# Moving the stores of a streaming add to a second DMA ring, with a smaller last chunk

## Chip, core and metric

The kernel runs on one core of one Trainium2 chip. The time is device microseconds from start to end of one execution. The profile's "span" leaves out a part of the launch, so it is about 1.8 us shorter than the time of the same execution (before: span 150.6 us, time 152.39 us).

## The reference

```python
# B, S, D = 512, 32, 640, bfloat16; alpha has one element
def reference(x, fx, alpha):
    return x + alpha * fx
```

Two arrays of 20.97 MB are read and one is written: 62.92 MB in all, and one multiply-add per element.

## The kernel before

The arrays are seen as 128 partitions of 81,920 columns, cut into five chunks of 16,384 columns (4 MB per array, 32 KB per partition row). Chunk k has an x tile (four buffers) and an f tile (two buffers); the result overwrites the x tile and is stored from it. In this text x2 is the load of x for chunk 2, f2 that of fx, c2 its compute, s2 its store; counting starts at 0, so "the third store" is s2. A "ring" is the queue of transfers of one issuing engine. Before, everything but alpha goes through one ring, that of SyncE:

```python
    load_x(0); load_f(0); load_x(1); load_f(1); load_x(2)
    compute(0)
    load_f(2);  store(0);  load_x(3)
    compute(1)
    load_f(3);  store(1);  load_x(4)
    compute(2)
    load_f(4);  store(2)
    compute(3)
    store(3)
    compute(4, 2)                     # last chunk in two halves
    store(4, 0, 2);  store(4, 1, 2)
    # (joined onto fewer lines here; compute is one VectorE instruction, or two halves)
```

## Time and profile before

| | before |
|---|---|
| time, median of 3 runs | 153.1 us (152.6 to 153.13) |
| span of the profile | 150.6 us |
| DMA engines moving data | 98.0% of the span = 147.6 us |
| DMA engines not moving data | 150.6 - 147.6 = 3.0 us |
| VectorE busy | 86.9 us (58%) |

DMA engines are the 16 units that move data between the chip's memory and the core. These are lines of the profile page of before. In the rows DVE (VectorE) and DMA each of the 40 figures stands for one fortieth of the span (3.8 us) and gives the busy share in tenths; the GB/s row gives what the DMA engines moved in it. A queue line gives packets, MB, and the time of its packets as a share of the span of the 16 DMA engines; q1 is the SyncE ring, q10 the ScalarE ring.

```profile
span 150.6 us, 85 instructions
...
DVE  0000009999679998499991006999900089997000
...
DMA  6999999999999999799999999999999999999994
GB/s 200 444 453 435 418 418 418 418 444 453 444 453 435 418 418 418 339 444 470 418 418 418 418 418 435 435 435 453 426 435 444 418 418 435 435 435 405 426 444 205
...
q1 hardware_dynamic: 2304, 62.92, 98.0%
q10 hardware_dynamic: 2, 0.00, 0.0%
```

DMA is at 9 in all but the first, last and one middle slice, while VectorE has long zeros. The bytes are fixed, so the DMA engines' rate bounds the kernel, and only the 3.0 us in which they do not work could be saved. Nearly all of these lie at the two ends: by the packet records, 1.7 us pass before the first row starts, and 1.2 us after the last one has ended.

The next lines are from the timeline of before (start us, duration us, engine, line, instruction, and in brackets how long the engine had been idle and what ended that).

```profile
62.24 17.28 DVE L69 SCALAR_TENSOR_TENSOR x_t<-f_t,a_f,x_t 128x16384 bf16<-128x16384 bf16 x1 [2.71 <-DMA f_t<-in_fx_dram]
...
120.91 17.42 DVE L69 SCALAR_TENSOR_TENSOR x_t<-f_t,a_f,x_t 128x8192 bf16<-128x8192 bf16 x2 [11.91 <-DMA f_t<-in_fx_dram]
```

The last load, f4, is in just before 120.91 us, and 17.42 us of compute follow. They cost nothing, because two whole stores (s2 and s3) stand in the ring behind f4 and keep the DMA engines busy while VectorE works.

### The profile page before, as it was taken

What the parts mean: (1) busy time and instruction counts of PE and PEld (TensorE: products, weight loads), DVE (VectorE), ACT (ScalarE), POOL (GpSimd) and SP (SyncE); (2) the same over time, 40 slices, a digit from 0 to 9 for tenths busy, and PEclk for the clock granted to TensorE, in tenths of its full rate; (3) what the DMA queues carried; (4) which work ended last, traced back from release to release, by engine and by line L of the source; (5) the groups of instructions that cost most, each with busy time, mean ns of one, the idle gap of its engine ahead of it and who ended that gap; (6) DMA issues with size and microseconds to landing.
All of it is one profiled execution on the core that took longest, in us unless ns stands there. A gap on an engine that the chain in (4) does not pass through costs nothing.

```text
span 150.6 us, 85 instructions
## 1 busy us (share of the span) xinstructions
PE 0.2 (0%) x1; PEld 0.1 (0%) x1; DVE 86.9 (58%) x8; POOL 0.2 (0%) x4
## 2 busy tenths in 40 slices
PE   0000000000000000000000000000000000000000
PEld 0000000000000000000000000000000000000000
DVE  0000009999679998499991006999900089997000
POOL 0000000000000000000000000000000000000000
DMA  6999999999999999799999999999999999999994
GB/s 200 444 453 435 418 418 418 418 444 453 444 453 435 418 418 418 339 444 470 418 418 418 418 418 435 435 435 453 426 435 444 418 418 435 435 435 405 426 444 205
DMA packets 2306, 62.92 MB, mean 418 GB/s; under 512 B 258, under 2 KB 258, under 8 KB 258
## 3 DMA queue, kind: packets, MB, share of 16 engines
q1 hardware_dynamic: 2304, 62.92, 98.0%
q10 hardware_dynamic: 2, 0.00, 0.0%
HBM read 41.94 MB, written 20.97 MB: 418 GB/s over the span
## 4 chain that ended last, share of the span: by engine, by line
DMA 56%; DVE 29%; DVEq 6%; issue 0%; SPq 0%
DMA f_t<-in_fx_dram 56%; DVE x_t L69 29%; DVEq L131 6%; SPq L59 0%; DVEq L69 0%
## 5 line engine op out<-in xcount | busy, mean ns | idle before, releaser
L69 DVE SCALAR_TENSOR_TENSOR x_t<-f_t,a_f,x_t 128x16384 bf16<-128x16384 bf16 (+1 forms) x6 | 86.6, 14439 | 49.5 <-DMA f_t<-in_fx_dram 49.5
L26 DVE COPY a_f<-a_ps 128x1 f32<-128x1 f32 x1 | 0.2, 159 | 1.1 <-PE a_ps L24 1.1
L22 DVE MEMSET ones<- 1x128 bf16 x1 | 0.2, 165 | 0.8 <-PEq L120 0.8
L24 PE MATMUL a_ps<-a,ones 1*128 1x1 bf16 x1 | 0.2, 159 | 1.9 <-DMA a<-in_alpha_dram 1.9
L120 POOL MEMSET const-bfloat16-1.0<- 128x1 bf16 x1 | 0.1, 102 | 0.0
L120 POOL MEMSET const-uint8-127<- 128x1 uint8 x1 | 0.1, 102 | 0.0
L24 PEld LDWEIGHTS <-ones 1*128 1x128 bf16 x1 | 0.1, 100 | 1.0 <-DVE ones L22 1.0
L120 POOL MEMSET const-float32-0.0<- 128x1 f32 x1 | 0.1, 99 | 0.2 <-issue 0.2
L120 POOL MEMSET const-float32-1.0<- 128x1 f32 x1 | 0.1, 99 | 0.0
## 6 DMA issues: line engine op xcount, KB each, us to landing
x_t<-in_x_dram SPq DMA_DIRECT2D x5, 4096.0 KB, 34.8
f_t<-in_fx_dram SPq DMA_DIRECT2D x5, 4096.0 KB, 32.1
out_dram<-x_t SPq DMA_DIRECT2D x4, 4096.0 KB, 36.5
out_dram<-x_t SPq DMA_DIRECT2D x2, 2048.0 KB, 15.2
a<-in_alpha_dram ACTq DMA_DIRECT2D x1, 0.0 KB
```

What stands on the lines that cost most here:

```text
L22: nc.vector.memset(ones[:], 1.0)
L24: nc.tensor.matmul(a_ps[:], ones[:], a_1[:], start=True, stop=True)
L26: nc.vector.tensor_copy(out=a_f[:], in_=a_ps[:])
L69: nc.vector.scalar_tensor_tensor(out=xt[k][:, s], in0=ft[k][:, s], scalar=a_f[:], in1=xt[k][:, s], op0=ALU.mult, op1=ALU.add,)
L120: nc = _bacc.Bacc("TRN2", target_bir_lowering=False, num_devices=1)
L131: with _tile.TileContext(nc) as tc:
```

## The change

The intent is to serve stores in rotation with loads, from a ring of their own, and to make the last chunks smaller so that less compute is left at the end. Only the third store is held, until the load f3 has landed. The diff, cut to its core:

```diff
-CHUNK = 16384
+SIZES = [16384, 16384, 16384, 16384, 8192, 8192]
 ...
-        nc.sync.dma_start(out=ov[...], in_=xt[k][:, bass.ts(j, n)])
+        st = nc.scalar.dma_start(out=ov[:, a : a + n], in_=xt[k][:, bass.ts(j, n)])
+        if behind is not None:
+            tc.add_manual_dep(st.ins, landed[behind].ins.name, ...)   # landed[k]: load_f(k)
 ...
     compute(2)
     load_f(4)
-    store(2)
+    load_x(5)
+    store(2, behind=3)
     compute(3)
+    load_f(5)
     store(3)
-    compute(4, 2)
-    store(4, 0, 2)
-    store(4, 1, 2)
+    compute(4)
+    store(4)
+    compute(5, 0, 2)
+    store(5, 0, 2)
+    compute(5, 1, 2)
+    store(5, 1, 2)
```

More of the change, by code (lines that the diff above doesn't have):

```diff
@@ L11 @@
 BF16 = mybir.dt.bfloat16
-CHUNK = 16384
+SIZES = [16384, 16384, 16384, 16384, 8192, 8192]
+STARTS = [sum(SIZES[:k]) for k in range(len(SIZES))]
+SLOT = max(SIZES)
 def alpha_to_lanes(nc, consts, psum, alpha, eng):
@@ L44 @@
     F = xv.shape[1]
-    K = F // CHUNK
-    assert K * CHUNK == F and K == 5
+    assert sum(SIZES) == F
     consts = ctx.enter_context(tc.tile_pool(name="consts", bufs=1))
@@ L54, with compute, store @@
     a_f = alpha_to_lanes(nc, consts, psum, alpha, nc.scalar)
-    xt, ft = {}, {}
+    xt, ft, landed = {}, {}, {}
     def load_x(k):
-        xt[k] = xs.tile([P, CHUNK], x.dtype, tag="x", name="x_t")
-        nc.sync.dma_start(out=xt[k][:], in_=xv[:, bass.ts(k, CHUNK)])
+        xt[k] = xs.tile([P, SLOT], x.dtype, tag="x", name="x_t")
+        nc.sync.dma_start(out=xt[k][:, : SIZES[k]], in_=xv[:, STARTS[k] : STARTS[k] + SIZES[k]])
     def load_f(k):
-        ft[k] = fs.tile([P, CHUNK], fx.dtype, tag="f", name="f_t")
-        nc.sync.dma_start(out=ft[k][:], in_=fxv[:, bass.ts(k, CHUNK)])
-    def compute(k, parts=1):
-        n = CHUNK // parts
-        for j in range(parts):
-            s = bass.ts(j, n)
-            nc.vector.scalar_tensor_tensor(
-                out=xt[k][:, s],
-                in0=ft[k][:, s],
-                scalar=a_f[:],
-                in1=xt[k][:, s],
-                op0=ALU.mult,
-                op1=ALU.add,
-            )
-    def store(k, j=0, parts=1):
-        n = CHUNK // parts
-        nc.sync.dma_start(
-            out=ov[:, k * CHUNK + j * n : k * CHUNK + (j + 1) * n],
-            in_=xt[k][:, bass.ts(j, n)],
-        )
+        ft[k] = fs.tile([P, SLOT], fx.dtype, tag="f", name="f_t")
+        landed[k] = nc.sync.dma_start(
+            out=ft[k][:, : SIZES[k]], in_=fxv[:, STARTS[k] : STARTS[k] + SIZES[k]]
+        )
+    def compute(k, j=0, parts=1):
+        n = SIZES[k] // parts
+        s = bass.ts(j, n)
+        nc.vector.scalar_tensor_tensor(
+            out=xt[k][:, s],
+            in0=ft[k][:, s],
+            scalar=a_f[:],
+            in1=xt[k][:, s],
+            op0=ALU.mult,
+            op1=ALU.add,
+        )
+    def store(k, j=0, parts=1, behind=None):
+        n = SIZES[k] // parts
+        a = STARTS[k] + j * n
+        st = nc.scalar.dma_start(out=ov[:, a : a + n], in_=xt[k][:, bass.ts(j, n)])
+        if behind is not None:
+            tc.add_manual_dep(
+                st.ins,
+                landed[behind].ins.name,
+                mybir.DependencyInfo(mybir.DependencyClass.Sync, mybir.DependencyReason.DATA),
+                reason="store behind a later load",
+            )
     load_x(0)
```

## The prediction

> **What bounds the kernel now.** The 16 DMA engines. The queue table gives the one data queue 98.0% of the 16 engines' span; the 40 slices show DMA at 9 in nearly every slice; 62.92 MB move in 150.6 us. A window of loads alone (10 to 20 us) runs at 433 GB/s, and the trace's packet records show one 32 KB row taking 1.213 us on its engine. Fifteen transfers of 4 MB are 15 x 8 x 1.213 = 145.6 us; with 1.7 us before the first byte, a slow first row, completion writes between transfers and about 1.2 us after the last, that is all of the span. VectorE is busy 86.9 us (58%) and hidden; the chain of waits runs through f landings and compute only because the single ring is always full. So there is at most about 1 us to gain, and anything that empties the rings costs time one for one.
>
> **What the change does.** Bytes are the same. Rows of 16 KB take 0.611 us (trace, last stores), so halving the last chunk costs about 0.3 us. Issue time moves from SyncE to the ScalarE queue (0.33 to 0.67 us each) and was never limiting. The Trainium skill, "DMA: Bandwidth & Descriptors", section "Issuing engines are not separate DMA queues", says transfers from both queues run on the same 16 engines and interleave; so I expect no bandwidth from the second ring (no trace here shows two rings yet).
>
> What changes is order. Before, the ring keeps two 4 MB stores (19.5 us of work) queued behind the last load, f4, which lands at 120.7 us; they cover both half computes (8.75 us each), and DMA never idles. After, each store is served while its following loads are: it takes its share early, f2 lands near 80 us instead of 62.2 (waits on f landings grow), later loads are late, and little store work is left behind the last load.
>
> I replayed both programs with these durations, one engine, issue-to-data 1.2 us, last-row-to-wait 1.1 us. The replay of before gives 149.8 us (measured 150.6). For after it depends on how an engine shares two rings, which this trace does not show:
> - a row from each in turn (32 KB store rows then get two thirds against 16 KB load rows): 158.3. The last load lands at 144.5, s3 and s4 are done by 145; then DMA idles about 6 us for the first 4.4 us half compute and issue, 2 us more before the last store.
> - a whole transfer in turn: 154.0, idle about 4 us at the tail.
> - bytes shared equally: 151.5, idle 1.5 us.
>
> The skill's same page, "Queues, rings and completion order", says engines round-robin between queues by packet, which fits the first or second best. Holding the third store behind f3 changes only the third case.
>
> **Prediction.** Adding 0.8 us of replay error and the 2.5 us between span and median time (153.1 less 150.6) gives 161.6, 157.3 and 154.8 us. I predict 157.5 us, 153.0 to 162.5 eight times in ten. Faster by over 2%: 0.02; within 2%: 0.42; slower by over 2%: 0.56.
>
> **What would show it.** Two data queues, DMA share falling from 98% to 93-96% with the loss in the last two or three of the 40 slices and 9s before; VectorE's third compute starting near 80 us, not 62; per-row time still 1.21 us; the chain of waits ending in two half computes of 4.4 us, each followed by an exposed store; the last f landing 137 to 145 us.
>
> **What would make it wrong.** Two rings moving more than 433 GB/s together (then faster), or less, from mixing reads and writes (slower still); stores getting a smaller share than loads, so that two of them remain queued at the last load's landing and hide the tail (same).

## The result

| | before | after |
|---|---|---|
| time, median of 4 runs each | 153.12 us (152.6 to 153.66) | 160.56 us (160.25 to 161.11) |
| span of the profile | 150.6 us | 158.5 us |
| DMA moving data: share of the span, us | 98.0%, 147.6 | 93.3%, 147.9 |
| DMA not moving data | 3.0 us | 10.6 us |
| VectorE busy | 86.9 us | 87.1 us |

The change is slower: the ratio is 1.049, with a 95% interval of 1.0444 to 1.0536. A ratio here, and in the experiments, is the mean time of one kernel's fast runs over that of the other's fast runs of the same rounds, so it is not quite the ratio of the medians.

The last two DMA rows of the table hold nearly the whole result. The time in which the DMA engines work is the same within 0.3 us, with two rings or one; the time in which they do not grows by 7.6 us, and the span by 7.9 us. The same lines of the page, now of after:

```profile
span 158.5 us, 95 instructions
...
DVE  0000029999499990000069997499994980004970
...
DMA  7999999999999999999999999999999999993155
GB/s 240 422 414 438 447 422 422 447 455 397 397 389 405 438 447 438 397 455 438 430 422 447 438 414 438 401 471 397 438 418 488 422 405 438 409 438 128 66 230 234
...
q1 hardware_dynamic: 1728, 41.94, 62.5%
q10 hardware_dynamic: 1010, 20.97, 30.8%
```

DMA stays at 9 until the 36th slice. All the loss is in the last four: 3, 1, 5, 5. Under the first three of these VectorE shows 4, 9, 7: it is computing, and the DMA engines wait for it. The timeline of after, third compute and last two:

```profile
80.61 17.28 DVE L71 SCALAR_TENSOR_TENSOR x_t<-f_t,a_f,x_t 128x16384 bf16<-128x16384 bf16 x1 [21.10 <-DMA f_t<-in_fx_dram]
...
144.62 8.88 DVE L71 SCALAR_TENSOR_TENSOR x_t<-f_t,a_f,x_t 128x4096 bf16<-128x4096 bf16 x2 [14.66 <-DMA f_t<-in_fx_dram]
```

The third compute starts at 80.61 us instead of 62.24, because f2 now shares the engines with stores. The last load is in at 144.5 us instead of 120.7. This table by stretch of after shows what follows (columns: stretch, its length, busy us of PE, PEld, DVE and POOL with instruction counts, granted clock, DMA share, GB/s):

```profile
118.00:136.00 18.00, 0.00 (x0) 0.00 (x0) 9.35 (x2) 0.00 (x0) 1.00 1.00 429
136.00:145.40 9.40, 0.00 (x0) 0.00 (x0) 0.78 (x1) 0.00 (x0) 1.00 0.84 359
145.40:150.00 4.60, 0.00 (x0) 0.00 (x0) 4.60 (x2) 0.00 (x0) 1.00 0.03 11
150.00:152.60 2.60, 0.00 (x0) 0.00 (x0) 2.60 (x1) 0.00 (x0) 1.00 0.93 384
152.60:154.40 1.80, 0.00 (x0) 0.00 (x0) 0.90 (x1) 0.00 (x0) 1.00 0.08 32
154.40:158.50 4.10, 0.00 (x0) 0.00 (x0) 0.00 (x0) 0.00 (x0) 1.00 0.59 242
```

Up to 136 us the engines are full. At 145.4 us every earlier store is done, and they stand for 4.6 us until the first half compute (4.48 us from 144.62) is finished and its store has been issued. Then they stand 1.8 us more, until the second half is stored. Before 145.4 the share is 0.84, because the 16 engines do not finish together: 16 packets are in work at 143.5 us, 9 at 144.0 and 1 at 145.0.

How the engines share two rings can be read from the queue lines for a stretch in which both have work. First 44 to 58 us of after, where load rows and store rows are both 32 KB:

```profile
q1 hardware_dynamic: 88, 2.88, 49.9%
q10 hardware_dynamic: 88, 2.88, 47.7%
```

Then 105 to 115 us of after, where load rows are 16 KB and store rows are still 32 KB:

```profile
q10 hardware_dynamic: 91, 2.98, 69.0%
q1 hardware_dynamic: 95, 1.29, 30.3%
```

A packet here is one row, or the small completion that ends a transfer (on each engine, one after eight rows). The packet counts of the two rings are equal within 5%; the bytes are not. An engine takes as many packets from one ring as from the other, so the ring with rows twice as long gets a little over two thirds of the time.

Equal counts alone could also come from turns of a whole transfer, since the transfers here all have eight rows per engine. The packet records kept with the trace decide it. They do not name the engine, but the end of one packet can be matched in time with the start of the next (within 6 ns). From 46 to 58 us of after, 141 packets could be matched so, and the next packet was of the other ring in all 141; from 60 to 80 us in all 282. The turn is one row. Halving the last chunks halved the load rows against the 32 KB rows of s2 and s3, and so gave those stores more of the engines, exactly where they should have been left for later.

### The profile page after: what moved, and what is told of

Same layout as the page of the kernel before. It is cut to its first block, busy times and chain, and to the rows that moved or that the text cites. A ratio compares the mean times of both kernels' runs of the same rounds, so it can differ in the third digit from the quotient of the medians.

```text
span 158.5 us, 95 instructions
## 1 busy us (share of the span) xinstructions
PE 0.2 (0%) x1; PEld 0.1 (0%) x1; DVE 87.1 (55%) x9; POOL 0.2 (0%) x4
## 4 chain that ended last, share of the span: by engine, by line
DMA 68%; DVE 25%; DVEq 3%; SPq 1%; issue 0%
DMA f_t<-in_fx_dram 68%; DVE x_t L71 25%; DVEq L143 3%; SPq L60 1%; SPq L64 0%; DVEq L71 0%
## 5 line engine op out<-in xcount | busy, mean ns | idle before, releaser
L71 DVE SCALAR_TENSOR_TENSOR x_t<-f_t,a_f,x_t 128x16384 bf16<-128x16384 bf16 (+2 forms) x7 | 86.8, 12407 | 64.4 <-DMA f_t<-in_fx_dram 64.4
## 6 DMA issues: line engine op xcount, KB each, us to landing
f_t<-in_fx_dram SPq DMA_DIRECT2D x4, 4096.0 KB, 40.2
```

The costliest lines, as they stand in the source:

```text
L71: nc.vector.scalar_tensor_tensor(out=xt[k][:, s], in0=ft[k][:, s], scalar=a_f[:], in1=xt[k][:, s], op0=ALU.mult, op1=ALU.add,)
```

## The experiments

Theory A: bytes and rate are the same, and the loss is DMA idle time at the end; stores served in turn with loads, row for row, leave too little store work behind the last load to cover the last compute. Rivals: the smaller chunks cost the time (B); the engines take whole transfers in turn, which alters the size (C); two rings together move less, or VectorE's longer waits on f are the loss (D). "Expected" texts call these A to D too; their "replay" is the one that the prediction describes.

In this table "DMA busy" is the sum of the two queues' shares of the span, times the span, and "not busy" is the rest. Times are medians, with the ratio to before and its interval.

| run | time us | ratio (95%) | span | DMA busy | not busy |
|---|---|---|---|---|---|
| before | 153.12 | 1 | 150.6 | 147.6 | 3.0 |
| after | 160.56 | 1.049 (1.0444 to 1.0536) | 158.5 | 147.9 | 10.6 |
| sizes alone | 153.46 | 1.0044 (0.9989 to 1.01) | 151.4 | 148.1 | 3.3 |
| ring alone | 165.55 | 1.082 (1.0783 to 1.0857) | 163.8 | 147.7 | 16.1 |
| no hold | 160.8 | 1.0502 (1.0458 to 1.0545) | 159.1 | 148.0 | 11.1 |
| s2 behind f4 | 153.24 | 1.0012 (0.9979 to 1.0046) | 151.4 | 147.6 | 3.8 |
| s2 behind x4 | 157.44 | 1.0298 (1.0253 to 1.0342) | 155.3 | 147.8 | 7.5 |
| store rows halved | 152.33 | 0.9963 (0.9925 to 1.0001) | 150.5 | 147.9 | 2.6 |
| load rows halved | 158.96 | 1.0405 (1.035 to 1.046) | 157.1 | 148.8 | 8.3 |
| load rows halved, halves swapped | 161.78 | 1.0555 (1.0538 to 1.0572) | 160.0 | 149.3 | 10.7 |
| stores by half the partitions | 175.83 | 1.1466 (1.142 to 1.1511) | 172.8 | 162.3 | 10.5 |

### The sizes alone

```diff
 # the change, with
-        st = nc.scalar.dma_start(...)
+        st = nc.sync.dma_start(...)
-    store(2, behind=3)
+    store(2)
```

> The chunk sizes of the change, but every store back on the SyncE ring behind the loads. Theory A (what costs is that stores are served in turn with loads by row, so little store work is left behind the last load): the ring never empties, replay 150.1 us of span, time 152.5 to 153.8, within 0.5% of before. Rival B (the smaller chunks and the two small last stores cost the time): near 160 us.

Measured: 153.46 us, not told apart from before. Rival B falls: by themselves the smaller chunks and the two small last stores cost 1% at most (the interval ends at 1.01), where the change costs 4.9%.

### The second ring alone

```diff
 # the kernel before, with
-        nc.sync.dma_start(out=ov[...], in_=xt[k][...])
+        nc.scalar.dma_start(out=ov[...], in_=xt[k][...])
```

> The kernel before with its five chunks, only the stores moved to the ScalarE ring, no hold. Theory A with turns by row: span 163.7 us, time 165 to 167, slower than the change, because both half computes (8.75 us each) stand bare at the end. Turns by whole transfer (rival C): span 155.2, time about 157. If the ring is harmless (rival B): about 153.

Measured: 165.55 us, span 163.8 against 163.7 for turns by row and 155.2 for turns by transfer. Rival C falls here, as it does in the packet records above. These are the VectorE and DMA rows of its page (here a slice is 4.1 us):

```profile
DVE  0000039998699950000399982999900000999920
...
DMA  7999999999989989999899999999999999007466
```

After 34 slices at 7 to 9 come two slices of zero, below the first half compute, and then four partly filled ones. The half computes are 8.75 us each here and 4.4 us in the change, and DMA's idle time follows them: 16.1 us against 10.6. So the smaller last chunks of the change do shorten the bare tail; they repair part of what the ring does.

### The hold taken away

```diff
-    store(2, behind=3)
+    store(2)
```

> The change without the hold on the third store. Theory A, by row: span 158.3, as with the hold (the hold delays the store by about 2 us, and by its landing nothing else waits on it), so within 0.5% of the change, 159.8 to 161.3 us. If the hold were what costs: faster than the change by several us. If it protects something: slower.

Measured: 160.8 us; the intervals of the two ratios to before (1.0502 and 1.049) overlap. The hold as it stands does next to nothing: c2, which s2 needs anyway, ends at 97.9 us in the change, and f3 is in at 101.2.

### The same hold, one f load later

```diff
-    store(2, behind=3)
+    store(2, behind=4)
```

> The change with one number altered: the third store waits for the fifth f load (f4), not the fourth. Two rings, small chunks, early stores and the late third compute (near 80 us) all stay. Theory A: more store work is left behind the last load, so the tail is covered: span 150.1, time 152.3 to 154. Rival D (two rings together move fewer bytes per second, or the late f2 and VectorE's longer waits are the loss): stays near 158 to 160.

Measured: 153.24 us, which is the time of before. This run decides between A and D. Two rings, small chunks and early first stores are all still there. The timeline of this run, third compute and last two:

```profile
80.85 17.29 DVE L71 SCALAR_TENSOR_TENSOR x_t<-f_t,a_f,x_t 128x16384 bf16<-128x16384 bf16 x1 [21.16 <-DMA f_t<-in_fx_dram]
...
137.59 8.88 DVE L71 SCALAR_TENSOR_TENSOR x_t<-f_t,a_f,x_t 128x4096 bf16<-128x4096 bf16 x2 [9.99 <-DMA f_t<-in_fx_dram]
```

Its DMA row:

```profile
DMA  6999999999989999999999999999999989999975
```

The third compute is as late as in the change (80.85 against 80.61), with the same wait of 21 us before it. That wait, the largest in both traces, costs nothing. What moved is s2, which was issued at 111.41 us instead of 101.29, and with it the last load: it is in at 137.5 us instead of 144.5. So 7 us more of store work lie behind it, and the DMA engines stay 96% busy under the last compute (137.6 to 146.5 us). DMA busy time is 147.6 us: two rings together lose no rate.

### A hold in between

```diff
-    store(2, behind=3)
+    store(2, behind=("x", 4))      # x4 is one 2 MB load after f3; load_x now notes its landing too
```

> The change with the third store held behind x4, one 2 MB load later than f3. A dose between the change and the hold behind f4. Theory A by row: span 156.4 (2 us less than the change), time 157.8 to 159.3, DMA idle at the end about 6.4 us against 8.2. Turns by whole transfer: no gain over its 154.0. Shared by bytes: 150.1.

Measured: 157.44 us, between the two, as theory A has it: not busy 10.6, 7.5 and 3.8 us for the holds behind f3, x4 and f4. The work left behind can be counted in the packet records. Leaving out the last two stores, which must wait for the last compute, the store rows that started after the last load's rows had ended come to 0.3 us of work for the 16 engines in the change, 3.4 us with s2 behind x4 and 7.5 us with s2 behind f4. So 3.1 and 7.2 us more store work were left at the end, and the time not busy fell by 3.1 and 6.8 us.

The gain was larger than expected (157.44 us, not 157.8 to 159.3; span 155.3, not 156.4). In the replay a store's rows took their turns 1.2 us after its issue. In the trace of the change, s0 is issued at 40.14 us, while loads are queued, and between 40.2 and 44.4 us the queue lines have only this:

```profile
q1 hardware_dynamic: 67, 1.67, 114.0%
```

No store row has started 4 us after the issue. (Packets count where they start and their whole duration with them, so a short stretch can exceed 100%.) A later entry leaves more store work for the end, which is the direction of this miss and of the next run's. How much of either it explains was not tested, nor why the entry is late.

### Store rows halved

```diff
-    store(0)
+    store(0, 0, 2)
+    store(0, 1, 2)           # likewise stores 1 to 4; store 2 still behind f3
```

> The change with every large store issued as two transfers of half the columns, so its rows are 16 KB where load rows are 32 KB; the order is not touched. By row, stores then get one third of the bytes against 32 KB load rows (half of them in the change) and one half against 16 KB load rows (two thirds in the change): more store work is left at the end, span 152.5, time 154 to 156, third compute starting near 71 us instead of 80.6. If the share does not follow the row size: no gain, 160.

Measured: 152.33 us, below the 154 to 156 expected (span 150.5, not 152.5). No order and no hold was altered, only the length of the store rows and, with it, the number of transfers (the last experiment takes these two apart), and all of the loss is gone. The queue lines of this run, 60 to 95 us (load rows 32 KB, store rows 16 KB):

```profile
q1 hardware_dynamic: 336, 9.96, 65.9%
q10 hardware_dynamic: 348, 5.18, 34.5%
```

And 105 to 130 us (both 16 KB):

```profile
q10 hardware_dynamic: 369, 5.52, 51.5%
q1 hardware_dynamic: 368, 5.24, 49.0%
```

Packet counts are equal again, and the stores' share of the time fell from one half to one third, and from two thirds to one half. The timeline shows the effect on the loads:

```profile
71.05 17.29 DVE L71 SCALAR_TENSOR_TENSOR x_t<-f_t,a_f,x_t 128x16384 bf16<-128x16384 bf16 x1 [11.60 <-DMA f_t<-in_fx_dram]
...
136.89 8.88 DVE L71 SCALAR_TENSOR_TENSOR x_t<-f_t,a_f,x_t 128x4096 bf16<-128x4096 bf16 x2 [10.70 <-DMA f_t<-in_fx_dram]
```

The third compute starts at 71.05 us (expected: near 71), and the last load is in at 136.8 us, so the tail is covered.

This was the only kernel with a median below that of before, so it was run once more:

> The fastest kernel so far once more (152.33 against 152.79 us, interval 0.9925 to 1.0001), with more rounds, to tell a gain of half a percent from none. Theory A: DMA never idles in either kernel, so the same within 0.5%.

Measured: 152.33 us against 153.3, ratio 0.9939 (0.9925 to 0.9952). That is 0.6% under before, small but clear in these rounds, where theory A expected at most 0.5%. No cause is shown: the two profiled executions have spans of 150.5 and 151.1 us, on both sides of the 150.6 of before.

### Load rows halved, and its confound

```diff
-        nc.sync.dma_start(out=xt[k][:, : SIZES[k]], ...)
+        for j in range(2): nc.sync.dma_start(out=xt[k][:, bass.ts(j, SIZES[k] // 2)], ...)
         # likewise for f
```

> The reverse: every load issued as two transfers of half the columns, stores as in the change. By row, stores get two thirds of the bytes in every shared stretch: still less store work left behind the last load, span near 160.1, time 161 to 163, so 1% slower than the change. If the share does not follow row size, or many small loads make no difference: as the change, 160.5. The extra issues can add waits for earlier transfers; if they show in the profile the size is off.

Measured: 158.96 us, 1% faster than the change where 1% slower was expected. The shares are as expected. This is 105 to 114 us of the run, with 8 KB load rows against 32 KB store rows; the stores move five times the bytes on an about equal number of packets (not four times, since the completions of the loads take turns too):

```profile
q10 hardware_dynamic: 105, 3.44, 88.5%
q1 hardware_dynamic: 98, 0.67, 17.8%
```

But the edit had done something else as well. With f5 in two transfers, the first half compute needs only the first of them. In the timeline of this run it starts earlier than in the change, at 143.57 us:

```profile
143.57 8.88 DVE L75 SCALAR_TENSOR_TENSOR x_t<-f_t,a_f,x_t 128x4096 bf16<-128x4096 bf16 x2 [13.66 <-DMA f_t<-in_fx_dram]
```

So the next run kept the loads and swapped the two halves, so that the first compute needs the transfer that lands last:

```diff
-    compute(5, 0, 2)
-    store(5, 0, 2)
     compute(5, 1, 2)
     store(5, 1, 2)
+    compute(5, 0, 2)
+    store(5, 0, 2)
```

> The run with halved load rows was 159.0 us, faster than the change and not slower as expected. Its edit also let the first half compute of the last chunk start when half of the last f load was in (it started at 143.6 us, while that load's second transfer landed about 2 us later). Here the two half computes (and their stores) are swapped, so that the first one needs the transfer that lands last; loads and rows are as in that run. Theory A: the early start is worth 2 to 2.6 us; span 159 to 160, time 160.5 to 162, so at or above the change. If halved load rows really help: stays at 159.

Measured: 161.78 us, span 160.0, and its timeline:

```profile
146.44 8.88 DVE L75 SCALAR_TENSOR_TENSOR x_t<-f_t,a_f,x_t 128x4096 bf16<-128x4096 bf16 x2 [15.61 <-DMA f_t<-in_fx_dram]
```

The last computes start 2.9 us later than in the run before it, and the span is 2.9 us longer: that was the early start. What is left is 0.6% slower than the change by the ratios (1.0555 to 1.049, timed in different calls). The direction is that of theory A, but the place is not: the time not busy is 10.7 us against 10.6 in the change, and the difference lies in the DMA busy time (149.3 us against 147.9). With only 0.3 us of earlier store work left behind the last load in the change, little more could be lost. Both runs also issue loads differently: the second half of x4 was issued at 81.79 and 82.58 us, after a wait of SyncE, where the change issued all of x4 at 64.97. So these two runs confirm the shares, and show nothing about the tail.

### Stores by half the partitions: a control that brought its own cost

```diff
 # from the run with halved store rows: stores 0 to 4 cut by partitions, not by columns
+        h = P // parts                # 64
+        st = nc.scalar.dma_start(out=ov[j * h : (j + 1) * h, a : a + n],
+                                 in_=xt[k][j * h : (j + 1) * h, :n])
```

> Control for the run with 16 KB store rows (152.3 us): the large stores are again issued as two transfers each, in the same order, but cut by partitions (64 each), so rows stay at 32 KB (16 KB for chunk 4). If it is row size that sets a ring's share: share in the shared stretches stays one half and two thirds, as in the change; time 159.0 to 161.5, like the change, with VectorE's third compute near 80 us. If it is the number of transfers (or the smaller units themselves): near 152 to 154.

Measured: 175.83 us, far outside both expectations. As a control of the share it still speaks: this is 44 to 60 us, with as many transfers as in the run with halved store rows, but with 32 KB rows.

```profile
q10 hardware_dynamic: 100, 2.75, 50.8%
q1 hardware_dynamic: 93, 2.82, 46.9%
```

The share is one half, as in the change, and the third compute starts at 82.15 us, not near 71. So it is the rows and not the number of transfers that moved the share. (It also speaks against turns by transfer: these stores have four rows per engine and transfer against the loads' eight, and still got half of the packets.) As a timing it tells nothing about the tail, since DMA busy time rose from 147.9 to 162.3 us: store rows ran longer (in the packet records the 32 KB store rows took 1.55 us on average instead of 1.21; in the stretch of 52 to 56 us, one of the worst, their median was 2.26). Stores on 64 partitions cost bandwidth here; why was not tested.

## Why the prediction was right

- **How sure it was.** Not very. The odds given were 0.56 for slower by over 2% and 0.42 for no such difference, and the range of 153.0 to 162.5 us took in all three rules of sharing. That the time fell inside it says little by itself; what was foreseen is the mechanism below, for one of three rules.
- **The bound.** Right. DMA busy time is 147.6 to 148.1 us in before, in the change and in every run that keeps whole load rows and 128 partitions. No time was there to be gained beyond the 3.0 us of before.
- **No bandwidth from a second ring.** Right. The Trainium skill, "DMA: Bandwidth & Descriptors", section "Issuing engines are not separate DMA queues", says that transfers of both issuers run on the same 16 engines and interleave. The traces agree: 147.6 us of DMA work with one ring, 147.9 with two.
- **Order, and the bare tail.** Right. The third compute was expected near 80 us and came at 80.61; the last f was expected between 137 and 145 and came at 144.5; the DMA share was expected at 93 to 96% and was 93.3%, with full slices before the end (the loss fell in the last four slices, where two or three were expected). The runs with the hold one load later (153.24 us) and in between show that the tail alone is the loss.
- **The rule of sharing.** The prediction left three open, so here it was not right but undecided. Turns by row is the one: the packet records show the two rings in alternation, row by row, and the replayed span was 158.3, measured 158.5; for the ring alone 163.7 and 163.8. The same page, "Queues, rings and completion order", has the engines go round-robin by packet and calls 9 to 17 descriptors typical for one. Before has 16 large transfers and 2304 packets on 16 engines, so nine packets (eight rows and a completion) per transfer and engine; with 9 to 17 a turn an engine would take a transfer at once. For these rows that does not hold: a turn was one row (141 of 141 matched), and the ring alone came to a span of 163.8 us instead of 155.2.
- **The size.** The 157.5 us lay between the sums for three rules, two of which do not hold, so it was 3 us low (measured 160.56); the sum for the rule that holds was 161.6. Within that sum the first idle stretch was over-estimated, about 6 us (from 145 on) against 4.6 (145.4 to 150.0): the earlier stores ended 0.4 us later than replayed, and the next store's rows started about 1 us sooner. The 0.8 us added for replay error were also not needed.
- **The hold.** The prediction said that it matters only if bytes are shared equally. They are not, and taking it away changed nothing that the intervals tell apart (160.8 us against 160.56).

## What to carry to other kernels

In a kernel bound by DMA, ask what is still queued when the last load lands: that work has to cover the last compute, and stores served early are missing there. When loads and stores got rings of their own here, the row length set each ring's share, so long store rows beside short load rows turned the priority around; shorter store rows (152.33 us), or one dependency that holds back a late store (153.24 us), put it right. Other sizes of rows were not tried. A long wait in the middle (21 us here) can be free while a wait of 4.6 us at the end is paid in full, so look at the last slices of the DMA row first; and when an edit splits a transfer, check what else may now start earlier.

## What the Trainium skill lacked or had wrong

- "DMA: Bandwidth & Descriptors", "Queues, rings and completion order": it gives turns by packet of some 9 to 17 descriptors, and no consequence of row size for the share. Here a turn was one row of 8 to 32 KB or one completion: two rings started about equal numbers of packets (88 and 88; 91 and 95; 105 and 98), so with rows of 1 to 1, 2 to 1 and 4 to 1 in length they moved bytes of 1 to 1, 2.3 to 1 and 5 to 1.
- The same page, "Latency and other measured facts", gives about 0.6 us to the first byte for transfers issued by SyncE or ScalarE. It does not say what to expect where another ring has loads queued: the first store of the change was issued at 40.14 us and its first row started at 44.6, 4.5 us later (3.6 to 5.2 us in the runs with two rings). At the end, with idle engines, a store issued at 149.13 us had its first row at 149.98, 0.85 us later.
- "Perfetto Trace Analysis", "DMA Optimizations", suggests one issuing engine for loads and another for stores where there are loops, to spread work more freely. It does not say what the order on one ring was worth: moving only the stores to a second ring cost 8.2% here. No page was found that says that store work queued behind the last load hides the last compute.
